# Attention, mixer and MLP on one core: the keys of a head taken in the order 16 p + c

## The chip, the core and the metric

The kernel runs on one of the eight cores of a Trainium2 chip, as one program. The figure is the device time of one execution in microseconds (us); less is better. A core has five engines, each with its own instruction stream: PE (matrix products and transposes, written PEld for its weight loads), DVE and ACT (elementwise work and reductions), POOL (small elementwise work) and SP, which here only issues transfers. A transfer (DMA) is carried out by 16 DMA engines that all streams share. SBUF is the on-chip memory of 128 partitions, PSUM the accumulators that PE writes, and DRAM holds inputs, outputs and one scratch tensor.

## The reference, cut to what matters

```python
x = A_x                                             # (1, 2048, 640)
mod = (silu(c) @ w_mod).reshape(1, 6, 1, 640)        # sa, ca, ga, sb, cb, gb
h = layernorm(x) * (1 + ca) + sa
x = x + ga * attention(h)                            # below
h = layernorm(x) * (1 + cb) + sb
x = x + gb * mixer_and_mlp(h)                        # B_w1 .. B_w4

def attention(h):                                    # 32 heads, 2048 queries, 2048 keys, head size 128
    q = (h @ wq), split into 32 heads
    scores = q @ k_cache.T * 128 ** -0.5             # k_cache, v_cache: (1, 32, 2048, 128), given
    p = softmax(scores)
    return heads_joined(p @ v_cache) @ wo
```

Everything is bf16 in memory. For each head, softmax and `p @ v` are sums over the 2048 keys. Such a sum does not depend on the order in which the keys stand, as long as scores, weights and values use one and the same order.

## The kernel before, in words

`Prog` records every operation with the keys that it reads and writes, and puts waits on semaphores where one engine needs another's result. On each engine the instructions stand in the order in which they were recorded, and no scheduler moves them.

The attention loop (lines 516 to 596) runs over `s = 16 h + j`: head h, and tile j of 128 queries. In step s:

- PE makes the scores of the tile in two halves of 1024 keys (`qk`, L286), from the transposed keys `KTs`, in which the 128 elements of a key lie along the partitions and the 2048 keys along the free axis. PSUM has room for one tile of scores.
- DVE copies each half to `negS`, with the sign changed, and takes its minimum in the same instruction (L559). PE can write a half again only when DVE has read it.
- POOL joins the two minima (L569), and ACT takes the exponential into a row of `Pb` (L572). `Pb` has 8 rows (`RPB`), so the exponential of step s writes over that of step s - 8 and has to wait until its transposition has landed.
- SP issues the transposition of `Pb` into `PTs` (12 rows) as a DMA (`transpose`, L222): six times a head for two tiles at once (1 MB), twice for one (512 KB). The tiles j = 3 and j = 10 are transposed on PE instead (`t_piece`, `t_evac`, L253 and L262), and one quarter of that is copied out by DVE (L264).
- 8 to 11 steps later PE multiplies the transposed weights with `Vaug` (`pv`, L299), 16 blocks of 128 keys. `Vaug[p, block, 0:128]` holds the values of one key in each partition, and a column of ones (129th of 130) gives the sum for softmax. ACT copies the result out (L550), POOL divides it (L447) and writes it to the scratch tensor in DRAM (L454).

SP's instructions of a head are eight transpositions of `Pb` and three loads for the heads to come: the keys of head h + 1 at j = 2 (`load_k`, L205), the query weights of head h + 2 at j = 6 (`load_wq`, L209) and the values of head h + 1 at j = 12 (`load_v`, L214). `KTs`, `wq` and `Vaug` have two buffers each. SP issues in program order, so whatever waits or takes long on it delays what stands behind. There is one queue for all of SP's transfers.

`load_k` is a transposing DMA. Its source is the head's (2048, 128) block of DRAM, 512 KB without gaps, whose rows of 256 B are one key each; column k of `KTs` becomes key k. `load_v` is a plain DMA that reads `(t p) d -> p t d`: partition p receives the keys p, 128 + p, 256 + p and so on, in 16 pieces of 256 B, which lie 32 KB apart in DRAM and 260 B apart in SBUF.

After the loop the scratch tensor is read back with eight transposing DMAs of 2 MB (`load_ot`, L495), whose source rows in DRAM are 16384 B long, and the projection with `wo` (L631), the mixer and the MLP follow.

Of the kernel before, what the change touches and what calls it, by code (L numbers as in the profile page):

```python
# [115 lines left out]
def bass_adaLN_cond__mha_block_cached__mixer_s_mlp__prompt_kernel(  # L116
# [6 lines left out]
    KT = D // 128  # L123
    NQT = SQ // 128
    NQC = SQ // 512
    NKT = SK // 128
# [11 lines left out]
    with ExitStack() as es:  # L138
# [11 lines left out]
        if True:  # L150
            with ExitStack() as es1:
# [22 lines left out]
                KTs = kv[:, 0:o1].rearrange("p (b s) -> p b s", b=2)  # L174
                Vaug = kv[:, o1:o2].rearrange("p (b k d) -> p b k d", b=2, k=NKT)
# [25 lines left out]
                G = Prog(nc, es1, "a")  # L201

                def load_k(h):
                    hb = h % 2
                    G.dma("sync", lambda e: e.dma_start_transpose(KTs[:, hb], A_k_cache[0, h]), ("k", hb), w=[("KT", hb)])  # L205

                def load_wq(h):
                    hb = h % 2
# [2 lines left out]

                def load_v(h):
                    hb = h % 2
                    G.dma("sync", lambda e: e.dma_start(Vaug[:, hb, :, 0:128], A_v_cache[0, h].rearrange("(t p) d -> p t d", p=128)),  # L214
                          ("v", hb), w=[("V", hb)])

                assert RPB % 2 == 0 and RPT % 2 == 0 and NQT % 2 == 0
# [108 lines left out]
                for cc in range(2, NQC):  # L326
                    load_x(cc)
                load_wq(0)
                load_k(0)
                load_v(0)  # L330
                load_mod(1, wmodr, 2 * D, 6 * D)
                if H > 1:
                    load_wq(1)
                    load_k(1)
# [172 lines left out]
                for g in range(NG):  # L507
                    d = max(PVE, min(PVD, PVE + (NG - 12 - g) // 2))
# [7 lines left out]
                for s in range(at[-1] + LAG + 1):  # L516
                    h, j = divmod(s, NQT)
# [9 lines left out]
                    for half in range(2):  # L527
# [10 lines left out]
                        if h + 1 < H and 2 * j + half in QPIECE:  # L538
                            cc, q = QPIECE[2 * j + half]
# [28 lines left out]
                    if s < NG:  # L568
                        G.op("gpsimd", lambda g, r8=r8: g.tensor_scalar(  # L569
                            out=nm[:, r8:r8 + 1], in0=nm0[:, r8:r8 + 1], scalar1=nm1[:, r8:r8 + 1], scalar2=None, op0=ALU.min),  # L570
                            r=[("nmh", 0, r8), ("nmh", 1, r8)], w=[("nm", r8)])
                        G.op("scalar", lambda a, s=s, r8=r8: a.activation(  # L572
                            Pb[:, s % RPB, :], negS[:, s % 3, :], ACT.Exp, bias=nm[:, r8:r8 + 1], scale=-1.0),
                            r=[("negS", s % 3), ("nm", r8)], w=[("Pb", s % RPB)])
                        if not is_pe(s):
                            if s % 2 == 1 and not is_pe(s - 1):
                                transpose(s - 1, 2)
                            elif s % 2 == 1 or is_pe(s + 1):
                                transpose(s, 1)
                        if j == 2 and h >= 1 and h + 1 < H:  # L580
                            load_k(h + 1)
                        if j == 6 and h + 2 < H:
                            load_wq(h + 2)
                        if j == PVD + 1 and h + 1 < H:
                            load_v(h + 1)
# [109 lines left out]
                for n in range(KT):  # L695
                    lst = []
                    p = 0
                    while p < 128:
# [8 lines left out]
                        p = pe_  # L707
# [136 lines left out]
```

## Time and profile before

| | us |
|---|---|
| median of 3 runs | 1614.81 |
| lowest, highest | 1610.35, 1619.43 |
| the profiled execution | 1604.1 |
| its span, from the first to the last instruction | 1602.3 |

The engines' busy time in that span: PE 1492.6 us (93%), DVE 1392.5 (87%), ACT 1288.2 (80%), POOL 622.8 (39%). The granted clock of PE is 0.993 of full speed on average.

| stretch of the span | what runs |
|---|---|
| 0 to 64 us | loads, first layer norm, queries of head 0, first steps |
| 64 to 1250 us | the attention loop |
| 1250 to 1602 us | reading the scratch back, projection, mixer, MLP |

How to read the profile: a group of instructions is named by its line in the kernel, its engine and operation, and the tiles that it writes and reads. A DMA's "issue" is SP's instruction, its "landing" the moment when all its data are written. SP's instruction for a transposing DMA lasts as long as SP is held by it, the wait ahead of it included. The busy share of the DMA engines can go over 1, because packets overlap on an engine. The queue of SP's transfers is q1, that of POOL's q0.

### The profile page before, as it was taken

The numbers are of one execution on the slowest core, as the hardware profiler recorded it, in microseconds if no ns is written. First come the engines' busy times: TensorE is split into PE (matmuls) and PEld (weight loads), VectorE is DVE, ScalarE is ACT, GpSimd is POOL, SyncE is SP. The second block draws the span as 40 slices with busy tenths as digits, with TensorE's granted clock in tenths as the row PEclk, the third lists the DMA queues.
The fourth block names the chain that finished last, engine by engine and source line by source line (L and its number), as shares of the span: only waits on it lengthen the run. The fifth ranks groups of instructions, "written<-read, shape, count | busy, mean of one in ns | idle before, by whom it ended". The sixth has DMA issues, their size and how long they took to land.

```text
span 1602.3 us, 34804 instructions
## 1 busy us (share of the span) xinstructions
PE 1492.6 (93%) x13978; PEld 963.0 (60%) x14231; DVE 1392.5 (87%) x2460; ACT 1288.2 (80%) x1145; POOL 622.8 (39%) x1394
## 2 busy tenths in 40 slices
PE   5799999999999999999999999999999799999998
PEld 3466666666666666666666666666666555545444
DVE  6999999999999999999999999999999266666424
ACT  4999999999999999999999999999999300055330
POOL 0144444444444444444444444444444423322000
PEclk9999999999999999999999999999999899999999
DMA  9999999999999999999999999999999994530000
GB/s 305 229 230 239 238 243 237 253 241 240 237 237 233 239 237 237 239 239 247 243 250 246 250 239 235 246 228 239 236 244 244 241 196 106 106 111 1 17 17 34
DMA packets 1167730, 333.62 MB, mean 208 GB/s; under 512 B 1148304, under 2 KB 1161552, under 8 KB 1167568
## 3 DMA queue, kind: packets, MB, share of 16 engines
q1 hardware_dynamic: 1161424, 314.59, 98.3%
q0 software_dynamic: 6144, 16.79, 3.3%
q8 instruction: 112, 1.84, 0.5%
q14 instruction: 50, 0.41, 0.1%
HBM read 43.48 MB, written 19.40 MB: 39 GB/s over the span
## 4 chain that ended last, share of the span: by engine, by line
DVE 30%; ACT 24%; PE 20%; DMA 15%; issue 10%; POOL 0%; SPq 0%; ACTq 0%; DVEq 0%
DVE negS L559 27%; ACT ring L572 19%; DMA ring<-ring 13%; PE Sps L631 8%; PE Sps L772 4%; PE Oaug L756 2%; PE QPp L756 2%; ACT ring L262 2%; ACT Of L550 2%; PE Sps L741 1%; ACT kv L244 1%; DMA ring<-in_A_x_dram 1%; DVE ring L364 1%; DMA negS<-o_scratch 1%; PE Sps L286 1%
## 5 line engine op out<-in xcount | busy, mean ns | idle before, releaser
L559 DVE TENSOR_SCALAR_CACHE_REDUCE negS<-Sps 128x1024 f32<-128x1024 f32 x1024 | 1177.2, 1220 | 22.2 <-PE Sps L286 12.5
L572 ACT ACTIVATE ring<-negS,small 128x2048 bf16<-128x2048 f32 x512 | 1011.4, 2029 | 21.9 <-DMA ring<-ring 15.7
L299 PEld LDWEIGHTS PTp<-kv,ring 128*128 128x128 bf16 x8192 | 560.0, 98 | 245.0 <-DMA ring<-ring 6.7
L286 PE MATMUL Sps<-kv 128*128 128x512 bf16 x1949 | 596.3, 383 | 62.8 <-DVE negS L559 42.9
L299 PE MATMUL PTp<-kv,ring 128*128 128x129 bf16 x8192 | 645.6, 221 | 6.5 <-DMA ring<-ring 5.6
L569 POOL TENSOR_SCALAR small<-small 128x1 f32<-128x1 f32 x512 | 145.8, 285 | 621.5 <-DVE negS L559 621.4
L286 PEld LDWEIGHTS Sps<-kv 128*128 128x128 bf16 x2048 | 124.5, 97 | 187.2 <-DVE negS L559 158.0
L447 POOL TENSOR_SCALAR On<-Of,small 128x128 bf16<-128x128 f32 x512 | 189.8, 371 | 13.0
L669 ACT COPY kv<-PTp 128x640 bf16<-128x640 bf16 x32 | 22.0, 692 | 155.0 <-PE PTp L666 154.9
L440 POOL TENSOR_TENSOR small<-Of,small 128x4 f32<-128x4 f32 x128 | 133.2, 1040 | 6.3 <-ACT Of L550 6.2
L454 POOL DMA_DIRECT2D o_scratch<-On x128 | 103.1, 806 | 40.8 <-POOL On L447 37.2
L237 PE MATMUL Oaug<-hTx,kv 128*128 128x512 bf16 x265 | 101.2, 387 | 7.9 <-ACT ring L262 4.2
L550 ACT COPY Of<-PTp 128x259 f32<-128x259 f32 x256 | 99.5, 389 | 10.5 <-PE PTp L299 10.5
L237 PE MATMUL QPp<-hTx,kv 128*128 128x512 bf16 x259 | 97.5, 381 | 2.5 <-ACT hTx L391 1.8
L559 DVE DVE_READ_ACCUMULATOR negS<-Sps 128x1 f32 x1024 | 85.4, 83 | 0.0
L612 POOL TENSOR_SCALAR On<-On 128x1 f32<-128x1 f32 x48 | 24.3, 507 | 152.9 <-DVE On L621 152.9
L639 DVE TENSOR_TENSOR ring<-Sps,mod_bc 128x640 f32<-128x640 f32 x16 | 13.2, 825 | 77.0 <-PE Sps L631 77.0
L631 PE MATMUL Sps<-wo,hTx 128*128 128x128 bf16 (+1 forms) x504 | 71.8, 304 | 5.0 <-DMA hTx<-o_scratch 4.7
L776 DVE TENSOR_TENSOR ring<-Sps,ring 128x640 f32<-128x640 f32 x16 | 13.2, 825 | 66.2 <-PE Sps L772 66.2
L631 PE MATMUL Sps<-wo,negS 128*128 128x128 bf16 (+1 forms) x504 | 69.1, 298 | 1.3 <-DMA negS<-o_scratch 0.9
L262 ACT COPY ring<-Oaug 128x1024 bf16<-128x1024 bf16 x64 | 66.2, 1034 | 0.0
L631 PEld LDWEIGHTS Sps<-wo,hTx 128*128 128x128 bf16 x512 | 40.2, 99 | 36.9 <-DMA hTx<-o_scratch 4.5
(82 smaller groups left out, 1011.2 us busy)
## 6 DMA issues: line engine op xcount, KB each, us to landing
kv<-in_A_v_cache_dram SPq DMA_DIRECT2D x32, 512.0 KB, 5.2
o_scratch<-On POOLq DMA_DIRECT2D x128, 128.0 KB, 4.5
ring<-in_A_x_dram SPq DMA_DIRECT2D x8, 640.0 KB, 4.9
kv<-in_A_wq_dram SPq DMA_DIRECT2D x32, 160.0 KB, 3.6
wo<-in_A_wo_dram SPq DMA_DIRECT2D x1, 5120.0 KB, 16.4
ring<-ring SPq DMA_TRANSPOSE x256, 7.1
ring<-in_w_mod_dram SPq DMA_DIRECT2D x1, 3200.0 KB, 13.6
out_dram<-wo SPq DMA_DIRECT2D x16, 160.0 KB, 1.8
```

Of the source, the lines that this page charges most:

```text
L237: G.op("tensor", lambda t: t.matmul(JB[jb], wq[:, hb, q, :], hT[:, q, cc * 512:(cc + 1) * 512], start=(q == 0), stop=(q == KT - 1)), r=[(" ...
L262: G.op("scalar", lambda a: a.copy(dst, src), r=[("J", jb)], w=[("PT", g % RPT, r)])
L286: ins = t.matmul(Sps[:, col:col + 512], QT[:, hb, j * 128:(j + 1) * 128], KTs[:, hb, col:col + 512], start=True, stop=True)
L299: ins = t.matmul(ob[:, 0:129], PTs[:, b, kt, :], Vaug[:, hb, kt, 0:129], start=(kt == 0), stop=(kt == NKT - 1))
L440: G.op("gpsimd", lambda g: g.tensor_tensor(out=rl[:, 4 * b:4 * b + 4], in0=Of[:].rearrange("p a z d -> p (a z) d")[:, 4 * b:4 * b + 4, 128 ...
L447: G.op("gpsimd", lambda g: g.tensor_scalar(out=On[:, b, z, :], in0=Of[:, 2 * b + z // 2, z % 2, 0:128], scalar1=rl[:, 4 * b + z:4 * b + z ...
L454: G.dma("gpsimd", lambda e: e.dma_start(o_scr[jj // 2:jj // 2 + 2, :, hh].rearrange("a p z d -> p a (z d)"), On[:, b].rearrange("p (a z) d ...
L550: G.op("scalar", lambda a, p=p: a.copy(Of[:, p % 4].rearrange("p z d -> p (z d)")[:, 0:259], PO[:, (p % 2) * 512:(p % 2) * 512 + 259]), r= ...
L559: G.op("vector", lambda v, half=half, s=s, r8=r8: v.tensor_scalar(out=negS[:, s % 3, half * 1024:(half + 1) * 1024], in0=Sps[:, half * 102 ...
L569: G.op("gpsimd", lambda g, r8=r8: g.tensor_scalar(out=nm[:, r8:r8 + 1], in0=nm0[:, r8:r8 + 1], scalar1=nm1[:, r8:r8 + 1], scalar2=None, op ...
L572: G.op("scalar", lambda a, s=s, r8=r8: a.activation(Pb[:, s % RPB, :], negS[:, s % 3, :], ACT.Exp, bias=nm[:, r8:r8 + 1], scale=-1.0), r=[ ...
L631: ins = t.matmul(YB[b][:, c0:c0 + cw], OTj[pr % 2][:, 2 * hh + z, :], wo[:, hh, c0:c0 + cw], start=(hh == 0), stop=(hh == H - 1))
```

## The change

The keys of a head are taken in another order. Position 128 c + p among the 2048 positions of a head, that is partition p of block c, now holds key 16 p + c in place of key 128 c + p. Both loads are rewritten for it, and nothing else is touched: the softmax and the products see the same keys in another order.

```diff
 def load_k(h):
     hb = h % 2
-    G.dma("sync", lambda e: e.dma_start_transpose(KTs[:, hb], A_k_cache[0, h]), ("k", hb), w=[("KT", hb)])
+    G.dma("sync", lambda e: e.dma_start_transpose(
+        KTs[:, hb].rearrange("p (c q) -> p c q", c=NKT), A_k_cache[0, h].rearrange("(q c) d -> q (c d)", c=NKT)), ("k", hb), w=[("KT", hb)])
...
 def load_v(h):
     hb = h % 2
-    G.dma("sync", lambda e: e.dma_start(Vaug[:, hb, :, 0:128], A_v_cache[0, h].rearrange("(t p) d -> p t d", p=128)),
+    G.dma("sync", lambda e: e.dma_start(Vaug[:, hb, :, 0:128], A_v_cache[0, h].rearrange("(p t) d -> p t d", t=NKT)),
           ("v", hb), w=[("V", hb)])
```

For the keys, the head's 512 KB of DRAM are now seen as 128 rows of 4096 B, with 16 consecutive keys in a row, and the transposing DMA takes 16 blocks of 128 columns from them. This is the form that the transpositions of `Pb` and `load_ot` have. For the values, partition p receives the keys 16 p to 16 p + 15, which are 4096 B without a gap in DRAM; in SBUF they still are 16 pieces of 256 B at a distance of 260 B. Number, size, place in the program and semaphores of the transfers are the same as before.

## The prediction, made before the result was known

> **What bounds the kernel now.** I read the page first: DVE is busy 87% of the span, the chain that ended last is led by DVE and ACT, and SP's queue holds 98.3% of 16 engines' time.
>
> ```profile
> span 1602.3 us, 34804 instructions
> q1 hardware_dynamic: 1161424, 314.59, 98.3%
> L559 DVE TENSOR_SCALAR_CACHE_REDUCE negS<-Sps 128x1024 f32<-128x1024 f32 x1024 | 1177.2, 1220 | 22.2 <-PE Sps L286 12.5
> L572 ACT ACTIVATE ring<-negS,small 128x2048 bf16<-128x2048 f32 x512 | 1011.4, 2029 | 21.9 <-DMA ring<-ring 15.7
> kv<-in_A_v_cache_dram SPq DMA_DIRECT2D x32, 512.0 KB, 5.2
> kv<-in_A_k_cache_dram SPq DMA_TRANSPOSE x32, 4.6
> ```
>
> The exponential (L572) has little idle time, but most of it is ended by a transposition of `Pb`. When in the loop? The DVE copy L264 runs once a head, and single heads can be taken as windows (columns: stretch, length, busy PE, PEld, DVE, ACT, POOL, clock, DMA share, GB/s):
>
> ```profile
> L264 DVE COPY ring<-QPp x32: 684/686/690, 58.2 to 1230.3; 128x1024 bf16<-128x1024 bf16 x32
> ...
> 226.00:263.22 37.22, 35.76 (x369) 24.22 (x373) 37.22 (x66) 37.22 (x32) 17.44 (x40) 1.00 1.21 243
> 488.72:527.41 38.69, 36.55 (x371) 24.88 (x376) 37.58 (x68) 36.94 (x31) 17.71 (x41) 1.00 1.26 231
> ```
>
> So there are two regimes. In head 5 (226 us) DVE has no gap: 37.22 us is its floor, and heads 1 to 9 all take just that. Head 12 (488.72) takes 38.69, and DVE is idle for 1.1 of it. From 58.2 to 1230.3 are 31 heads in 1172.1 us; 31 times 37.22 is 1153.8, so **18.3 us are lost to the second regime**. Its chain of waits, with SP's own instructions beside it:
>
> ```profile
> 570.59 9.84 DMA ring<-ring
> 580.51 1.30 ACT ring L572
> 581.82 8.48 DMA ring<-ring
> 590.38 2.31 ACT ring L572 x2
> 602.02 8.11 DMA ring<-ring
> 610.60 9.35 DMA ring<-ring
> ```
> ```profile
> 590.10 2.48 SPq L205 DMA_TRANSPOSE kv<-in_A_k_cache_dram  x1
> 592.62 4.40 SPq L222 DMA_TRANSPOSE ring<-ring  x1
> 597.06 0.58 SPq L209 DMA_DIRECT2D kv<-in_A_wq_dram  x1
> 597.68 12.25 SPq L222 DMA_TRANSPOSE ring<-ring  x3
> ```
>
> The chain goes from a transposition to the exponential that overwrites its row, then to the next transposition. SP issues back to back: each starts within 0.05 us of the end of the one before. In the trace, the pair of tiles 4 and 5 lands 5.6 us after its exponential in head 0, 9.9 in head 1, 13.3 in head 4, 13.9 in head 8, 15.3 in head 12. From that landing to the exponential that reuses the row there are 9.3 us in head 0, 0.4 in head 8 and 0.1 in head 12. The queue falls behind by (13.9 - 5.6) / 8 = 1.0 us a head while DVE still sets the pace. From head 10 on the slack is gone and the queue sets it. Its need is then 37.22 + 1.0 = 38.3 us a head; the starts of heads 11 to 16 are 38.7 apart on average.
>
> **What the two loads cost in that queue.** DMA rate in short windows (same columns), first the after-loop transposition from DRAM rows of 16384 B, then transpositions of `Pb`, then a window with the K load, then one with V:
>
> ```profile
> 1299.00:1302.00 3.00, 2.95 (x21) 1.59 (x20) 2.40 (x4) 0.00 (x0) 0.00 (x0) 1.00 1.28 290
> 581.00:583.00 2.00, 2.00 (x27) 1.49 (x25) 2.00 (x5) 2.00 (x2) 0.62 (x2) 1.00 1.28 290
> 591.00:593.00 2.00, 2.00 (x22) 1.33 (x20) 2.00 (x5) 2.00 (x2) 0.50 (x2) 1.00 1.13 202
> 611.00:614.00 3.00, 2.69 (x25) 1.65 (x25) 2.85 (x7) 3.00 (x2) 1.43 (x3) 1.00 1.21 220
> 36.00:44.00 8.00, 7.17 (x33) 3.13 (x33) 4.28 (x8) 5.98 (x6) 0.59 (x2) 1.00 1.06 396
> ```
>
> Transpositions run at 290 GB/s both from SBUF and from wide DRAM rows; with K or V in the window the rate falls to 202 and 220. The last window is the load of `wo`, pieces of 1280 B.
>
> **The change part by part.** Order, waits and semaphores of all instructions stay; nothing moves. Only the two loads' own time changes.
>
> *K.* Its 2048 packets of 256 B stay. By the trace K lands 2.10 us (median of 30) after the transfer ahead of it, a single-tile transposition of the same size 1.77 (median of 45). The new form is that of `load_ot`: 524288 B at 290 GB/s are 1.81 us. I take a gain of 0.3 us a head. Bounds: at 202 GB/s K now takes 2.6 us, so up to 0.8 gained; the slowest `load_ot` held SP 11.62 us for 2 MB, 2.9 us for 512 KB, so up to 0.8 lost. I stay near 1.81, since two rows of the same form show it.
>
> The nearest rule speaks against me. The Trainium skill, "DMA: Bandwidth & Descriptors", section "Latency and other measured facts", gives DMA transposes 261 GB/s with a non-contiguous middle dimension against some 350 to 400 when contiguous. By it K would go from about 1.5 us to 2.0, an estimate from that page, and lose 0.5 us a head. The trace disagrees: the contiguous source has 202 in its window, the strided one 290.
>
> *V.* It lands 2.58 us (median of 31) after the transfer ahead of it. The built program still writes 16 pieces of 256 B a partition, so I do not take the 396 GB/s of 1280 B pieces, which would be 1.32 us, but the 290 of the 256 B packets: 1.81, a gain of 0.8 us. Bounds: nothing gained, if the pieces in SBUF set the pace, up to 1.3 gained. SP's issue of V (0.58 us) may change; another copy's issue is 0.33 to 0.58 where nothing holds it, so I allow 0.3 us either way and take 0.
>
> *First and last heads.* K and V of head 0 are issued at 9 and 16 us. The chain up to 44 us runs over the loads of x, DVE and PE, so nothing comes of it. After the loop the chain runs through POOL's last writes; 0 to 3 us could follow from an earlier last transposition, and I take 0.
>
> *Sum.* The queue needs 1.1 us a head less: 38.3 to 38.7 becomes 37.2 to 37.6, against a floor of 37.22. The excess of 0 to 0.4 us over 30 heads is 0 to 12 us, of which the first 8 (9.3 of slack in head 0 less about 1) cost nothing: a loss of 0 to 4, and I take 3. Of the 18.3 us, 15.3 come back: 1604.1 - 15.3 = 1588.8 us on the profiled execution. The median of the runs shown is 10.7 us above that execution. Since the lost time hangs on small delays in a queue, I take the difference as more of the same loss, which goes too, and add 1 us: **1590**. If the difference is a fixed part, it is 1599.5. Late next is DVE, in every head, so a larger saving gives no more than 1604.1 - 18.3 = 1586.
>
> **The rivals.**
>
> 1. *Nothing is saved.* The pieces of 256 B in SBUF set V's pace and K stays at 2.1 us. For it: neither size nor number of written pieces changes. Against it: the same pieces pass at 290 GB/s in two other rows. Time as before, 1604 to 1615, say 1613.
> 2. *Strided rows make K slower.* Successive rows 4096 B apart could meet in DRAM, and the queue, which has no room from head 10 on, passes every extra microsecond to the exponential. At 2.9 us K costs 0.8 more; with V's gain at half, 0.4, the net is 0.4 us over 30 heads, 12 us; with none, 24. That is 1616 to 1628 on the profiled execution, 1627 to 1639 at the median, say 1630. It decides from about 2.8 us: 0.4 for V and 8 us / 30 heads above 2.1. Against it: rows of 16384 B go at 290. The rule of the Trainium skill quoted under K ("DMA: Bandwidth & Descriptors") would do the same through 0.5 us, and the 202 of the contiguous source speaks against that.
>
> **How the numbers follow.** About 0.5% (8 us) is what a measurement of this kernel can tell from no change. Chances: the forecast 0.63, with its own range 1583 to 1603; rival 1 0.22; rival 2 0.15. Faster takes 0.61 of the forecast and 0.03 of rival 1; same takes 0.02, 0.18 and 0.03; slower the rest, 0.01 and 0.12. The range goes from 1583 to 1620: it holds the forecast but for 0.05 and rival 1, and leaves rival 2 out.
>
> **What would show it.** If I am right, the windows with K and V show 260 GB/s and more, heads stay at 37.22 us to the end, the exponential's idle time by transpositions falls from 15.7 us to under 5, and L264 goes from first to last in 1154 to 1158 us. If V's landing stays near 5.2 us and K's near 4.6 from issue, rival 1 holds; K above 5.4, rival 2. It would also be wrong if the queue's need came from its stops and not from these two loads, since their gain would then be taken up by waiting elsewhere.

## The result and the profile after

The changed kernel takes 1619.37 us (median of 14 runs, 1613.81 to 1627.61), the kernel before, on the same chip, 1612.04 us (14 runs, 1603.12 to 1619.43). The ratio is 1.0052, 95% interval 1.0031 to 1.0073: 7 to 8 us slower. The forecast was 1590. The time still lies inside the stated range of 1583 to 1620, but by 0.6 us and because that range was drawn to hold rival 1; the direction was forecast the other way.

The two profiled executions are 21.7 us apart (1604.1 and 1625.85), since the one of before is among the fastest of its kernel and the one of after among the slowest. So the profiles tell where the time is lost, and the medians how much. From the page of the changed kernel, whose lines after L203 stand one further down:

```profile
span 1624.1 us, 34804 instructions
q1 hardware_dynamic: 1161424, 314.59, 98.8%
q8 instruction: 112, 1.84, 0.5%
L560 DVE TENSOR_SCALAR_CACHE_REDUCE negS<-Sps 128x1024 f32<-128x1024 f32 x1024 | 1180.3, 1226 | 38.2 <-PE Sps L287 20.4
L573 ACT ACTIVATE ring<-negS,small 128x2048 bf16<-128x2048 f32 x512 | 1007.4, 2016 | 39.2 <-DMA ring<-ring 33.2
kv<-in_A_v_cache_dram SPq DMA_DIRECT2D x32, 512.0 KB, 5.1
```

SP's queue carries the same packets (1161424) and is a little fuller. The exponential's idle time that a transposition ends is 33.2 us, where it was 15.7. The single lines of the DVE copy, of K and of V in the changed kernel (shortest, median and longest instruction in ns, first and last start in us):

```profile
L265 DVE COPY ring<-QPp x32: 685/689/722, 58.3 to 1249.5; 128x1024 bf16<-128x1024 bf16 x32
...
L205 SPq DMA_TRANSPOSE kv<-in_A_k_cache_dram x32: 1856/2098/10822, 8.9 to 1214.8; - x32
...
DMA to landing us min/median/max: 4.4/4.9/12.9
...
L215 SPq DMA_DIRECT2D kv<-in_A_v_cache_dram x32: 588/597/657, 16.1 to 1234.2; - x32
...
DMA to landing us min/median/max: 4.8/5.1/6.8
```

From 58.3 to 1249.5 are 1191.2 us for 31 heads, 37.4 above DVE's floor of 1153.8, where it was 18.3. From issue to landing K takes 4.9 us (4.6 before) and V 5.1 (5.2). Measured from the landing of the transfer ahead, in the trace and as medians, K went from 2.10 to 2.44 us and V from 2.58 to 2.96 (K without heads 0 and 1, V without head 0). Windows of the changed kernel, first head 5, then head 12, then 2 us with K's load and 3 us with V's (columns as in the prediction):

```profile
226.00:263.22 37.22, 35.77 (x368) 24.22 (x373) 37.22 (x66) 37.22 (x33) 17.49 (x40) 1.00 1.18 245
513.32:552.89 39.57, 36.21 (x367) 24.59 (x372) 37.57 (x66) 37.33 (x32) 17.50 (x40) 1.00 1.20 236
519.30:521.30 2.00, 1.95 (x22) 1.33 (x20) 1.67 (x5) 2.00 (x2) 0.34 (x2) 1.00 1.02 230
499.50:502.50 3.00, 3.00 (x33) 1.95 (x30) 3.00 (x7) 3.00 (x2) 1.04 (x4) 1.00 0.95 205
```

The two regimes are there as before, and DVE's floor is the same 37.22 us. But the second begins earlier: the slack between the landing of tiles 4 and 5 and the exponential that reuses the row (9.3 us in head 0 of both kernels) is down to 0.3 us in head 4; before, it was 1.0 there and 0.4 in head 8. Heads after the sixth take 37.2 to 40.2 us. The rates are far from the 290 GB/s on which the forecast stood: 230 with K and 205 with V.

### The profile page after: what moved, and what is told of

Same layout as the page of the kernel before. It is cut to its first block, busy times and chain, and to the rows that moved or that the text cites. A ratio compares the mean times of both kernels' runs of the same rounds, so it can differ in the third digit from the quotient of the medians.

```text
span 1624.1 us, 34804 instructions
## 1 busy us (share of the span) xinstructions
PE 1495.3 (92%) x13978; PEld 965.2 (59%) x14231; DVE 1395.6 (86%) x2460; ACT 1290.1 (79%) x1145; POOL 624.8 (38%) x1394
## 3 DMA queue, kind: packets, MB, share of 16 engines
q1 hardware_dynamic: 1161424, 314.59, 98.8%
## 4 chain that ended last, share of the span: by engine, by line
ACT 28%; DMA 27%; PE 20%; DVE 17%; issue 7%; SPq 0%; POOL 0%; ACTq 0%; DVEq 0%; POOLq 0%
DMA ring<-ring 25%; ACT ring L573 23%; DVE negS L560 15%; PE Sps L632 7%; PE Sps L773 4%; ACT ring L263 2%; PE Oaug L757 2%; PE QPp L757 2%; ACT Of L551 2%; PE Sps L742 1%; ACT kv L245 1%; DMA ring<-in_A_x_dram 1%; DVE ring L365 1%; DMA negS<-o_scratch 1%; DMA o_scratch<-On 1%
## 5 line engine op out<-in xcount | busy, mean ns | idle before, releaser
L573 ACT ACTIVATE ring<-negS,small 128x2048 bf16<-128x2048 f32 x512 | 1007.4, 2016 | 39.2 <-DMA ring<-ring 33.2
L455 POOL DMA_DIRECT2D o_scratch<-On x128 | 103.1, 806 | 40.8 <-POOL On L448 37.2
L560 DVE DVE_READ_ACCUMULATOR negS<-Sps 128x1 f32 x1024 | 91.4, 89 | 0.0
L632 PEld LDWEIGHTS Sps<-wo,hTx 128*128 128x128 bf16 x512 | 40.2, 99 | 37.1 <-DMA hTx<-o_scratch 5.1
```

The source lines that it names most:

```text
L455: G.dma("gpsimd", lambda e: e.dma_start(o_scr[jj // 2:jj // 2 + 2, :, hh].rearrange("a p z d -> p a (z d)"), On[:, b].rearrange("p (a z) d ...
L560: G.op("vector", lambda v, half=half, s=s, r8=r8: v.tensor_scalar(out=negS[:, s % 3, half * 1024:(half + 1) * 1024], in0=Sps[:, half * 102 ...
L573: G.op("scalar", lambda a, s=s, r8=r8: a.activation(Pb[:, s % RPB, :], negS[:, s % 3, :], ACT.Exp, bias=nm[:, r8:r8 + 1], scale=-1.0), r=[ ...
L632: ins = t.matmul(YB[b][:, c0:c0 + cw], OTj[pr % 2][:, 2 * hh + z, :], wo[:, hh, c0:c0 + cw], start=(hh == 0), stop=(hh == H - 1))
```

## The experiments

Times are medians of 12 runs (14 for the first two rows, 4 without V), ratios go against the kernel before on the same chip. "Loop" is the time from the first to the last of the 32 DVE copies in the one profiled execution; it differs by several us between executions of one kernel and only supports the ratio.

| kernel | us | ratio, 95% interval | loop |
|---|---|---|---|
| before | 1612.04 | 1 | 1172.1 |
| the change | 1619.37 | 1.0052 (1.0031 to 1.0073) | 1191.2 |
| the change, another chip | 1621.4 | 1.0063 (1.0039 to 1.0088) | 1188.6 |
| K alone | 1610.09 | 0.999 (0.9967 to 1.0012) | 1182.5 |
| K alone, another chip | 1610.69 | 0.9992 (0.9976 to 1.0008) | 1175.9 |
| V alone | 1616.41 | 1.0019 (1.0000 to 1.0039) | 1184.2 |
| V alone, another chip | 1617.02 | 1.0039 (1.0022 to 1.0055) | 1184.1 |
| before, V's copy without its mark | 1616.32 | 1.0021 (1.0004 to 1.0038) | 1183.9 |
| the change, V in two copies | 1612.66 | 1.0012 (0.9992 to 1.0032) | 1176.0 |
| before, no V from head 2 on | 1586.12 | 0.9844 (0.981 to 0.9878) | 1154.0 |
| pairs of keys | 1607.42 | 0.9973 (0.9958 to 0.9987) | 1173.8 |
| before, V's pieces 384 B apart | 1608.24 | 0.9995 (0.9977 to 1.0014) | 1169.6 |
| the change, V's pieces 384 B apart | 1613.7 | 1.0027 (1.0008 to 1.0045) | 1179.3 |
| pairs and 384 B together | 1604.51 | 0.9977 (0.9959 to 0.9995) | 1174.1 |

**The loads by themselves.** A kernel issues each form of each load eight times in a row, and then in turn with a transposition of one tile:

```diff
+            section(k_old)
+            section(k_new)
+            section(v_old)
+            section(v_new)
+            section(v_old_plain)      # V as before, built without its mark
+            section(v_new_halves)
+            section(tr, k_old)
+            section(tr, k_new)
+            section(tr, v_old)
+            section(tr, v_new)        # ... and the other forms
```

What "mark" means: in the built program of the kernel before, SP's plain copies, all but the last piece of `B_w4`, carry a flag (`ant_dge_precooked`); POOL's copies have none. In the changed kernel V's 32 copies have lost it. Their source, 4096 B a partition without a gap, is merged by the build into 2048 pieces of 256 B in one dimension, and the flag is gone.

> The disputed loads by themselves: the kernel leaves out all of the computation (it copies x to the output) and issues on SP, eight times each and twice over, single-tile transpositions from SBUF, K in the old and in the new form, V in the old form, in the new form, in the old form with its copy unmarked, and in the new order as two marked copies of eight pieces; then each of these alternating with a single-tile transposition. In the built program a copy carries a mark when both sides have the same dimensions; the new V source collapses to 2048 rows and loses the mark. Theory A (the copy without the mark reaches the DMA engines later): V new and V old unmarked alternate with a transposition about 0.3 to 0.4 us slower per pair than V old marked, the two marked halves do not, and K old and K new are equal within 0.1 us. Theory B (rows 4096 B apart are slower to read): K new takes 0.3 us more than K old (2.1), and the V forms are equal or V new is faster by up to 0.8.

Windows of that kernel while nothing but one form of load runs: K as before, K changed, V as before, V changed, V as before without the mark (columns: stretch, length, busy DVE, busy POOL, clock, DMA share, GB/s):

```profile
36.00:50.00 14.00, 0.00 (x0) 0.00 (x0) 1.00 1.21 238
56.00:70.00 14.00, 0.00 (x0) 0.00 (x0) 1.00 1.13 225
76.00:91.00 15.00, 0.00 (x0) 0.00 (x0) 1.00 1.39 220
98.00:112.00 14.00, 0.00 (x0) 0.00 (x0) 1.00 1.39 221
119.00:133.00 14.00, 0.00 (x0) 0.00 (x0) 1.00 1.39 220
```

V goes at 220 GB/s whatever the order in DRAM, 2.36 us a load; its packets of 256 B take 25 ns each (median), those of a transposition 18. K gets slower by the change, not faster: 2.15 and 2.12 us became 2.41 and 2.27 (means of the distances between landings, the two repetitions). The single-tile transpositions by themselves, 512 KB each as well, land 2.46 and 2.47 us apart. What differs in V is the start. Where the queue is empty, the first packet of a marked V copy starts 1.04 us after SP's instruction does (both repetitions), of the changed one 1.46 and 1.38, of the unmarked one in the old order 1.40 and 1.41: without the mark a copy starts 0.34 to 0.42 us later, merged or not. Next SP's instructions of the same kernel where V alternates with a transposition: V as before (L138), changed (L142), unmarked (L148).

```profile
244.25 3.87 SPq L160 DMA_TRANSPOSE TD<-TS  x1
...
272.14 4.01 SPq L160 DMA_TRANSPOSE TD<-TS  x1
276.19 0.58 SPq L138 DMA_DIRECT2D VB<-in_A_v_cache_dram  x1
...
283.95 4.44 SPq L160 DMA_TRANSPOSE TD<-TS  x1
...
313.24 4.05 SPq L160 DMA_TRANSPOSE TD<-TS  x1
317.34 0.59 SPq L142 DMA_DIRECT2D VB<-in_A_v_cache_dram  x1
...
325.46 3.99 SPq L160 DMA_TRANSPOSE TD<-TS  x1
...
354.20 3.94 SPq L160 DMA_TRANSPOSE TD<-TS  x1
358.18 0.61 SPq L148 DMA_DIRECT2D VB<-in_A_v_cache_dram  x1
```

The first and the last transposition of each group are six pairs apart: 27.89 us for V as before, 29.29 changed, 28.74 unmarked, so 4.65, 4.88 and 4.79 us a pair. SP's own instruction hardly differs (0.58, 0.59, 0.61). The pair is longer though V alone is not. In the second repetition it is 4.69, 4.87 and 4.74. V in two marked copies has 4.81 and 4.77, no less than the unmarked one. K's pairs grow about as much or more, from 4.88 to 5.10 and from 4.61 to 4.97.

**K alone, V alone, and V without its mark.** These are the two halves of the change's diff, each by itself (keys and values then stand in different orders, so these two kernels compute something else), and the kernel before with this edit:

```diff
+                    def f(e):
+                        nc.dge_precook = False
+                        r = e.dma_start(Vaug[:, hb, :, 0:128], A_v_cache[0, h].rearrange("(t p) d -> p t d", p=128))
+                        nc.dge_precook = True
+                        return r
```

> K in the new form, V in the old one (scores and values then use different key orders, so the function computed changes, no time of an operation does). Theory A (only V's copy costs): same as before, ratio 0.998 to 1.002, K's median distance to the landing ahead stays near 2.1 us. Theory B (K's strided rows cost): the whole loss of the change or more, ratio 1.004 to 1.010, K's distance about 2.4 us. Both parts at half: 1.002 to 1.003.

> V in the new form, K in the old one (key orders differ between the two, as above). Theory A (V's unmarked copy starts late): ratio 1.004 to 1.008, the DMA rate right after V's issue falls to about 100 GB/s for 1 us. Theory B (K's rows): 0.997 to 1.000, since V is not slower and may gain.

> The kernel before, with V's old source and order but V's copy built without the mark. Theory A: the full loss of V without its gain, ratio 1.004 to 1.012, V's issue on SP a little longer, the queue's gap behind V longer by 0.3 us. Theory B, or if the mark does not matter: 0.998 to 1.002.

K alone costs nothing that can be measured, although its pairs above grew by 0.2 to 0.4 us: what a pair costs more does not carry over to the kernel one to one. V alone and the lost mark alone cost the same on the same chip, 1616.41 and 1616.32 us, with loops of 1184.2 and 1183.9, about half of the 0.004 that was the least expected. The lost mark is thus enough for what V's half cost there. That the new order and the merged source do nothing beside it is not shown: V lands 2.76 us after the transfer ahead of it without the mark, and 3.02 with V's whole half (2.58 before). The exponential's group of the unmarked kernel:

```profile
L576 ACT ACTIVATE ring<-negS,small 128x2048 bf16<-128x2048 f32 x512 | 1008.6, 2019 | 32.5 <-DMA ring<-ring 26.4
```

Both halves were measured again on another chip, with much the same outcome (table):

> K's new form alone, once more, since the first comparison (0.999, 0.9967 to 1.0012) does not fit the loads by themselves, where K new costs 0.25 us more behind a transposition: over the 21 heads in which the queue sets the pace that is 5 us. If it shows in the kernel: 1.002 to 1.004. If the queue absorbs it: 0.998 to 1.001 again.

> V's new form alone, once more (first 1.0019, 1.0000 to 1.0039; by the loads themselves 0.23 us more behind a one-tile transposition, 5 to 7 us over the loop). If it is the larger part of the change's 1.0052 and 1.0063: 1.003 to 1.005. If both parts are needed for the loss: 1.001 to 1.002.

**The whole change, with V's mark kept.** The changed kernel was taken again, beside one that loads V in two copies of 8 pieces. Their sources can't be merged, and both have the mark.

```diff
+                    for z in range(2):
+                        G.dma("sync", lambda e, z=z: e.dma_start(
+                            Vaug[:, hb, 8 * z:8 * z + 8, 0:128], A_v_cache[0, h].rearrange("(p t) d -> p t d", t=NKT)[:, 8 * z:8 * z + 8]),
+                            ("v", hb, z), w=[("V", hb, z)])
```

> The changed kernel once more, beside the runs below on the same chip. Its first comparison gave 1.0052 (1.0031 to 1.0073), while K's new form alone gave 0.999 (0.9967 to 1.0012) and V's alone 1.0019 (1.0000 to 1.0039), together 1.001. If the parts add up, 1.000 to 1.003 here; if the two loads hurt each other in the queue, 1.004 to 1.007 again.

> The changed kernel with V's load as two copies of eight pieces each, which keep the mark (key order and K's form as in the change). By the loads alone, a pair of transposition and V took 4.63 us old, 4.89 new, 4.67 in halves. Theory A (V's unmarked copy with its merged source is the loss): 0.15 to 0.25 us a head back, 5 to 8 us, ratio 0.998 to 1.002. Theory B (K's rows are the loss, by the loads alone 0.25 to 0.4 us a pair): stays at 1.003 to 1.006.

```profile
L575 ACT ACTIVATE ring<-negS,small 128x2048 bf16<-128x2048 f32 x512 | 1010.9, 2028 | 24.8 <-DMA ring<-ring 18.4
```

With the same key order and the mark, the loss is gone: 1.0012 where the change has 1.0063, on one chip, and the exponential waits 18.4 us for transpositions, near the 15.7 of before. Even so nothing is gained. Two things differ from the change here, the mark and two copies of half the size; no kernel here loads V in one marked copy of the new order. Nor do the pairs foretell it: the 4.67 for the halves in the expectation divides by another count of intervals than the 4.63 and 4.89 beside it, and with theirs it is 4.78.

**Without V.** To see what the queue costs at all, V is loaded for heads 0 and 1 only:

```diff
+                    if h > 1:
+                        return
```

> The kernel before without the V loads of heads 2 to 31; these heads use the values of heads 0 and 1, so that part of the result is left out. Theory (SP's DMA queue is what the loop waits for from head 10 on, and DVE's 37.22 us a head is the floor): 2.4 us a head less in the queue ends the second regime, 1586 to 1592 us, ratio 0.984 to 0.989, L264 from first to last in 1154 to 1157 us. Rival (the lost 18 us come from something else, ACT or the stops by code loading): 0.995 to 1.001.

From its page, and the line of its DVE copy:

```profile
q1 hardware_dynamic: 1099504, 298.85, 93.9%
DVE 57%; PE 20%; issue 16%; ACT 4%; DMA 2%; POOL 1%; SPq 0%
L574 ACT ACTIVATE ring<-negS,small 128x2048 bf16<-128x2048 f32 x512 | 1015.8, 2038 | 5.2 <-POOL small L571 5.2
```
```profile
L266 DVE COPY ring<-QPp x32: 683/720/747, 58.1 to 1212.1; 128x1024 bf16<-128x1024 bf16 x32
```

The loop takes 1154.0 us, 31 times 37.22 to 0.2 us, and no exponential waits for a transposition any more. The chain goes to DVE. So with V's 2.4 to 2.6 us a head out of SP's queue the second regime is gone, and 1586 us is the time without it. It also sizes the loss: 24.6 us at the medians of that chip.

**What sets V's pace.** The loads by themselves again, with V's pieces at other distances in SBUF, and in one piece of 4096 B a partition, alone and in turn with a two-tile transposition:

```diff
+                G.dma("sync", lambda e: e.dma_start(VB[:, i, 0:NKT * w].rearrange("p (t w) -> p t w", w=w)[:, :, 0:128],
+                                                    A_v_cache[0, h].rearrange("(t p) d -> p t d", p=128)), ("v", i), w=[("V", i)])
```

> Loads by themselves again (all computation left out), eight in a row: V in the old order with pieces of 256 B at a distance in SBUF of 256, 260 (as in the kernel), 272, 288, 320, 384 and 512 B; V in the new order at 256 and 288 B; then each of K old, K new and five V forms alternating with a two-tile transposition. V took 2.36 us in every form so far, with packets of 25 ns where those of transpositions take 18. Theory C (the 260 B distance, that is pieces that start off a 32 B boundary, sets V's pace): 1.8 us at 256, 288, 320, 384 and 512 B, 2.36 at 260, between at 272; the new order at 256 B, which is one piece of 4096 B on both sides, 1.3 to 1.4 us. Rival (any 256 B piece read from DRAM takes so long): 2.36 at every distance. K new against K old: 0.25 to 0.4 us more a pair, as in the first of these runs, or equal if that was scatter.

Windows with V alone, pieces 260, 384 and 512 B apart in SBUF, then one piece of 4096 B (columns as in the windows of the first such kernel):

```profile
34.00:50.00 16.00, 0.00 (x0) 0.00 (x0) 1.00 1.41 218
113.00:125.00 12.00, 0.00 (x0) 0.00 (x0) 1.00 1.27 288
130.00:146.00 16.00, 0.00 (x0) 0.00 (x0) 1.00 1.34 218
150.00:158.00 8.00, 0.00 (x0) 0.00 (x0) 1.00 1.02 407
```

So V's pace alone is set where it writes. 256, 260 and 512 B apart it takes 2.37 to 2.40 us, 320 B 2.08, 384 B 1.81 (the 290 GB/s of a transposition), and one piece 1.29. That 260 B are slow for being unaligned falls with this: 256 and 512 B are as slow. In turn with a two-tile transposition most of it is lost. SP's transpositions again, six pairs apart, in turn with V as before and then with V as the change has it:

```profile
307.13 6.21 SPq L151 DMA_TRANSPOSE TD<-TS  x1
...
348.69 6.22 SPq L151 DMA_TRANSPOSE TD<-TS  x1
...
365.21 6.44 SPq L151 DMA_TRANSPOSE TD<-TS  x1
...
406.33 6.24 SPq L151 DMA_TRANSPOSE TD<-TS  x1
```

V as before takes 6.93 and 6.92 us a pair (two repetitions), the single piece 6.53 both times. Of the 1.10 us that it is faster alone, 0.39 come through. From 260 to 288 B V alone gains 0.17, and the pair changes by less than 0.1 either way. V as the change has it takes 6.85 and 6.99: behind a transposition of two tiles its later start doesn't show, while behind one tile it did. In the kernel V stands behind one tile. K's pairs grow here too, from 7.16 and 7.11 to 7.38 and 7.40.

**Fewer, larger pieces.** With key 256 g + 2 p + z in place (z, g, p), V goes in 8 pieces of 512 B, 520 B apart, and K is transposed from rows of 512 B. Ones stand on both sides of a piece, so that the row sum comes in two columns, which POOL adds:

```diff
+                    G.dma("sync", lambda e: e.dma_start_transpose(
+                        KTs[:, hb].rearrange("p (z r) -> p z r", z=2), A_k_cache[0, h].rearrange("(r z) d -> r (z d)", z=2)),
...
+                    G.dma("sync", lambda e: e.dma_start(Vaug[:, hb, :, 2:258], A_v_cache[0, h].rearrange("(g p z) d -> p g (z d)", p=128, z=2)),
```

> A version built on the finding that V's 2048 pieces of 256 B are what V costs: keys in the order 256 g + 2 p + z, so that two neighbouring keys are one piece of 512 B on both sides (1024 pieces, the copy keeps its mark) and share a block of SBUF with a ones column on each side; the row sum comes in two columns, which POOL adds; PE clears the accumulator once for two tiles with a product of zeros; K is transposed from rows of 512 B. If pieces of 512 B at a distance of 520 B take 1.4 to 1.9 us a head in place of 2.36, the queue needs 0.5 to 0.9 us less and most of the 18 us come back: 1588 to 1600 us, ratio 0.986 to 0.993. Rival (the extra product and POOL's addition, or K's rows, take it back): 0.997 to 1.005.

It is faster than the kernel before, 0.9973, but by 4 us and not by 11 to 23. K lands 1.78 us after the transfer ahead of it (2.10 before). V lands after 2.96, later than the 2.58 before, though it has the mark and half as many pieces. PE also has a product of zeros more for two tiles. Which of these parts brings the 4 us was not separated.

**V's distance in the kernel.** The pieces 384 B apart need 12 KB in place of 8, and SBUF is full; V's buffers go into rows of `wo`, which are loaded later.

> The kernel before, old key order and old K, with V's pieces 384 B apart in SBUF in place of 260. Alone, such a load takes 1.81 us, at 260 B 2.39, at 256 B 2.37, at 512 B 2.39. For the room, V's two buffers lie in the last ten rows of the place of wo, and those rows of wo are loaded when the last values have been used, 0.8 MB shortly before the end of the loop and 0.8 MB after it, which may cost up to 4 us there. If V's time in the queue is what the loop waits for: 0.55 us a head less, 8 to 16 us back in the loop, 1596 to 1605 us, ratio 0.990 to 0.996. If the distance does not count beside the other traffic: 1.000 to 1.003. If the late part of wo costs more than thought: above 1.002 with the loop itself shorter (L264 from first to last under 1165 us).

This run (1624.91 us, 1.0018, 0.9994 to 1.0042) can't be read as time: the second late part of `wo` was ordered ahead of the last products of head 31, which waited 24.9 us for it and multiplied its rows in place of the values. Only V's landing can be used, 2.45 us. In the next form only V's buffer 0 lies in `wo`, five rows are loaded after the loop, and the last products see their values:

```diff
-                Vaug = kv[:, o1:o2].rearrange("p (b k d) -> p b k d", b=2, k=NKT)
+                VP, WV = 192, 5
+                Vaug = [x.rearrange("p (k d) -> p k d", k=NKT) for x in (
+                    wo[:].rearrange("p h n -> p (h n)")[:, (H - WV) * D:(H - WV) * D + NKT * VP], kv[:, o1:o1 + NKT * VP])]
...
                     if s == OT0:
                         load_ot(0)
+                        G.dma("sync", lambda e: e.dma_start(wo[:, H - WV:H], wos[:, H - WV:H]), "wo2", w=["wo2", ("V", 0), "ones0"])
```

> The kernel before, with the pieces of V 384 B apart in SBUF in place of 260 B. One V buffer lies in the last five rows of wo, which are loaded after the loop (0.8 MB, 2.7 us in the queue in e12, where it also had to be waited for 24.9 us by the last products; here it hasn't). Theory A (the distance of the pieces in SBUF sets V's pace in the loop as it does alone, 2.37 us at 260 B and 1.81 at 384): V lands about 2.0 us after the transfer ahead of it, the queue needs 0.5 us a head less, and half of the 18 to 25 us lost to the queue come back: 0.992 to 0.996 of before. Rival (in the loop V waits for the transpositions around it, and its own packets hardly matter, as the 2.45 us of e12 suggest): V stays at 2.4 to 2.6, 0.997 to 1.001.

> The whole change (both key orders), with the pieces of V 384 B apart as in e13. If the change's loss comes from V's copy starting later, since it has no mark in the built program, and from K's rows, it is there at this distance too: 0.004 to 0.006 above e13. If it comes from how the merged copy writes pieces 260 B apart, it is gone, and this equals e13 within 0.002.

> Key order 256 g + 2 p + z: K transposed from rows of 512 B, as in e9, where it landed 1.78 us after the transfer ahead of it against 2.10 before; V in two marked copies of 8 pieces each, 384 B apart. If K's gain of 0.3 us a head and V's of 0.2 to 0.5 add up, the queue's need falls to DVE's 37.2 us a head or just above: 0.986 to 0.992 of before, 1588 to 1600 us. If V gains nothing by the distance, it is like e9, 0.996 to 0.999.

The kernel before with 384 B, its exponential and its DVE copy:

```profile
L577 ACT ACTIVATE ring<-negS,small 128x2048 bf16<-128x2048 f32 x512 | 1013.1, 2035 | 19.9 <-DMA ring<-ring 14.6
```
```profile
L266 DVE COPY ring<-QPp x32: 685/687/690, 58.1 to 1227.6; 128x1024 bf16<-128x1024 bf16 x32
```

V lands 2.45 us after the transfer ahead of it (2.58 before), though alone it would be 0.58 faster. The time is unchanged, 0.9995; outside the loop this kernel has 3.5 us more than the one before (1603.3 - 1169.6 against 1602.3 - 1172.1), so the loop may have gained up to that much. The rival expectation held. The change at 384 B is 1.0027, 0.0032 above it, against 0.0052 and 0.0063 at 260 B: half of the loss or more is there at this distance too, as a copy without its mark would have it, but the intervals of the two overlap. Joining pairs and 384 B gives 0.9977, no more than pairs alone. Of the kernels that load everything it has the lowest median, 1604.51 us, but by the ratios pairs alone is as good.

## Why the prediction was wrong, point by point

1. *What bounds the kernel* was right. Two regimes, DVE's floor of 37.22 us and SP's queue behind it: without V the loop takes 1154.0 us against the 1153.8 worked out, and the kernel 1586.12 against the limit of 1586. That the 10.7 us between the profiled execution and the median are more of the same loss was right as well: taking the queue's excess away gained 24.6 us at the median and left four runs within 0.5 us of each other (1585.98 to 1586.49). The size of the queue's need was read too high: (13.9 - 5.6) / 8 spreads the first head's jump to 9.9 over eight heads, and from head 1 to 8 it is (13.9 - 9.9) / 7 = 0.6 us a head. Nor does the second regime last to the end: in the trace of before heads 19 to 25 take 37.2 to 37.7 us again.

2. *"V: 2.58 to 1.81, a gain of 0.8 us"* is the step that failed first and cost most. It took the 290 GB/s of other packets of 256 B for V's own limit. By itself V goes at 220 GB/s in both orders, 2.36 us and not 1.81, so its own bound "nothing gained, if the pieces in SBUF set the pace" was the case, and the mechanism of rival 1. Its counter-argument, that the same pieces pass at 290 GB/s in two other rows, compared transpositions, whose packets took 18 ns, with a copy's, which took 25.

3. *"SP's issue of V may change ... I take 0"* looked at the wrong cost. SP's instruction went from 0.582 to 0.597 us, so 0 was right for it. But a copy without its mark begins later, its first packet by 0.34 to 0.42 us; of this 0.18 to 0.23 us stay in the pair with a one-tile transposition, 0.05 to 0.14 by the mark alone. In the kernel the mark alone costs 3.4 us (0.0021 of 1612.42), as much as V's whole half on that chip. Of the built copy the prediction looked at the pieces that it writes, and not at how it is started.

4. *"K: 2.10 to 1.81, a gain of 0.3 us"* failed in sign, by little. Alone the changed K is 0.15 to 0.26 us slower, in turn with transpositions 0.2 to 0.4, within the bounds that were given (0.8 either way). The price of 1.81 us was the rate of chosen windows of 2 and 3 us: in the trace of before all 64 single-tile transpositions, 512 KB each, land 2.09 us after the transfer ahead of them in the median, like K, and by themselves 2.46 apart; the 1.77 given is of 45 of them. The rows it stood on, `load_ot` at 290 GB/s, are 2 MB from rows of 16384 B; rows of 4096 B are another case, which was not shown. In the kernel K alone is 0.999 and 0.9992, so rival 2's price was never paid; that the wrong sign cost nothing there was luck.

5. *The rule of the Trainium skill* weighed under K ("DMA: Bandwidth & Descriptors", section "Latency and other measured facts": 261 GB/s for a non-contiguous middle dimension, 350 to 400 contiguous) had the direction right and the forecast had it wrong. The sizes are not those: 225 and 238 GB/s in the windows above, 5% apart (7 and 12% by the landings of all eight), where the page would have 25% and more.

6. *The sum* took a load's gain alone for a gain of the queue. Even where V does get faster alone, by 0.58 us at 384 B or by 1.10 in one piece, little of it comes through between transpositions: 0.13 us in the landing and nothing measurable in the time, or 0.39 us in the pair. At 384 B V takes just the 1.81 us alone that were forecast, and the 15.3 us did not come back. The prediction's last sentence named a neighbour of this, that the gain would be taken up by waiting elsewhere.

7. *The signs* answered clearly: rates of 230 and 205 in place of 260, 33.2 us of waiting in place of under 5, a loop of 1191.2 in place of 1154 to 1158. V's 5.1 us from issue to landing pointed to rival 1; K's 4.9 lay between the two rivals.

What stays open: K alone costs nothing and V alone 0.0019 to 0.0039, but together it is 0.0052 and 0.0063. The intervals leave room for a plain sum on one chip; a way in which K's 0.15 to 0.26 us cost only once V's delay has used up the slack was not tested. So up to half of the loss has no cause shown. Why a copy without its mark starts later, and why 384 B apart is fast and 512 is not, the runs don't say.

## What to carry to other kernels

Before costing a rewritten DMA, compare what the build makes of both forms: a source that merges into one dimension lost a flag here and started 0.34 to 0.42 us later, though bytes and packets stayed. A rate seen on transfers of the same packet size is no price for a transfer of another kind; measure that form alone, then in turn with its neighbours, and then in the kernel, since in this full queue only part of what V gained alone came through, and what K lost in turn did not show at all. And take the load out once, as was done here with V, to learn what a perfect version could be worth before working on its shape.

## What the runs showed of the hardware that was not expected

- Behind V's issue the merged copy has a deeper dip of the DMA rate and then a higher peak. In the loop, averaged over 31 heads in stretches of 0.25 us, the rate from 1.25 us after V's issue is 213, 189, 175, 222, 248, 263 GB/s before, and 172, 127, 90, 107, 170, 222 in the changed kernel, which then reaches 283. The lost mark alone doesn't make this dip: in the old order without the mark it is 160, 171, 170, 209, 242, 265. And V in marked pieces of 512 B ("pairs of keys") has the deepest, down to 66, and reaches 341 after it. Why, no run here says.
- 512 KB loaded by themselves in pieces of 256 B take 2.36 to 2.40 us when the pieces are 256, 260 or 512 B apart in SBUF, and 1.81 us at 384 B. At 260 and 288 B in SBUF the pieces may be 256 B or 32 KB apart in DRAM with 0.04 us of difference at most.
- The instruction queue (q8, 112 packets of 16384 B, about 90 of them in the loop) coincides in the trace of before with stretches in which SP's queue moves little. Counted in steps of 0.25 us from 64 to 1230 us, SP's queue is under 60 GB/s for 160 us, and 97 of these lie within 1 us of such a packet, though these surroundings make up only 275 of the 1166 us. The 97 us are about 3 us a head, more than either load's whole gain as forecast. No run here took the packets away, so it is seen side by side only and not shown as a cause.
